# A new hand-written order for a convolution and SwiGLU kernel: transfers among the products, two splits later, another joined list

## The chip, the cores and the metric

The kernel runs on one core of one Trainium2 chip. The metric is the device time of one execution in microseconds (us). Three runs of the kernel before gave 2442.12, 2444.2 and 2449.53 us, median 2444.2. One more execution was profiled; it took 2447.03 us.

## The reference

`x` is (8, 4096, 192) in float32. Part one is a causal convolution over the sequence with 7 taps, one set of softmaxed taps for each of 8 heads (24 channels a head). Part two is a feed-forward block on the 32768 resulting rows of 192, with a hidden size of 1536:

```python
w = softmax(weight, axis=-1)                     # (8 heads, 7 taps)
out[b, s, h, :] = sum_k w[h, k] * x_pad[b, s + k, h, :]
x = out.reshape(32768, 192)
xn = x / sqrt(mean(x * x) + 1e-6) * rms_g
g, val = xn @ w_gate, xn @ w_val                 # 192 x 1536 each
y = (g * sigmoid(g) * val) @ w_out               # 1536 x 192
```

## The kernel before, in words

**Pairs.** The 32768 rows are done in 32 pairs of token blocks, two blocks of 512 rows each. Pair 0 and most of pair 1 have code of their own; pairs 2 to 31 all run the same program, shifted from pair to pair.

**Products.** Both matrix products of a pair are done by a scheme that saves products for sums (7 block products in the place of 8, and a like one for the gate and value product). What a program of a pair issues on TensorE is a list of 110 words, `LINE`. 68 gate words come first (`P1.0`, `Aa.1`, ...): each is six products of 64 x 128 weights with 512 columns (L948), three parts of a weight piece against three parts ("splits") of the tokens. The letters name the product, the digit one of six groups of hidden rows. Then 42 output words (`o1.1`, ...) follow, each twelve products (L976), which sum up in accumulators X, Y and Z.

**Ring.** The gate weights' 48 pieces (192 KB) of a pair are read again from DRAM for every pair, through a ring of 12 slots. When the last word that reads a slot has been issued, `ring_load` (L822) puts the load of the next piece into that slot on SP's queue. So a ring load waits for TensorE, and what is put on SP's queue behind it waits as well.

**Order by hand.** Nothing is planned at run time. `run` walks through `FIRST` (pair 1), `SECOND` (pair 2) and `ORDER` (pairs 3 on, one walk for each) and issues each word as it comes; every engine works its own words in this order, and waits where data or a buffer are missing. `p3` issues three words of `LINE`. Every other word names an engine (A ScalarE, V VectorE, G GpSimd, S the SP queue) and an act; a `+` behind it means one pair ahead, `++` two, `-` one pair behind:

- `f1`, `f3` (ScalarE copies), `f4`, `f5`, `f6` (VectorE sums, L1018 and L1025): from one bank of products to the next; `ga` to `gd`: silu of a bank (L1031), `ma` to `md`: silu times value (L1038), into the tiles `ht`; after both, the bank is free.
- `h1` to `h4` (L1003): the sums of `ht` that the output words read. `o6.j` reads `h2.j`, `o7.j` reads `h3.j`.
- `c1`, `s7`, `c2` (copies), `C22`, `C21` (sums, L1055), `T11` to `T22` (transposes into `o_sb`, L991), `st` (stores, L1087): the output. `C22` and `C21` free or change the accumulators that following words need.
- `cv0` to `cv6` (L470 on ScalarE for tap 0, else L474): the taps of the convolution, over all 128 partitions; `sq`, `red`, `pow`, `bc`, `mul`: the normalisation, of which GpSimd does `pow` and `mul` (L524).
- `pl` (put_away, L1098): eight transfers of the normalised rows to DRAM; `ft` (fetch, L676): four transfers back, turned, into the tokens `xb`; `ld` (load_part, L174): eight loads, one a head, of x for the convolution of the pair after, into the one buffer `xh` that `pl` has just emptied.
- `x1` to `x4` (L868): sums of the tokens; `n`, `l`, `d` (L705 on ScalarE, L854, L856): the three splits of the five token operands 0 to 4.

The walk is short to state:

```python
for word in words:
    p = w + word.count("+") - word.count("-")
    if word[0] == "p":
        for _ in range(int(word[1:].rstrip("+-"))):
            if p in pairs:
                next(pairs[p].line)
    ...
    else:
        eng, name = word[0], word[1:].rstrip("+-")
```

A product bank is one of four pairs of PSUM banks. `open` takes the first free one in the order in which `g`, `m`, `C21`, `T11` and `T12` gave them back, so the order of the words also settles which word waits for whose bank.

In `FIRST`, the token operands of pair 2 still lie where the ring's slots will be (the operand that the trace calls `ring`), so `R`, the start of the ring, waits for the last split that reads them, `Vd.0+`.

Of the kernel before, what the change touches and what calls it, by code (L numbers as in the profile page):

```python
# [20 lines left out]
def kernel(  # L21
# [58 lines left out]
    )  # L80
    ORDER = (
# [15 lines left out]
    )  # L97
    SECOND = (
# [15 lines left out]
    )  # L114
    FIRST = (
# [14 lines left out]
    )  # L130
    LINE = (
# [7 lines left out]
    )  # L139

    cst = ctx.enter_context(tc.tile_pool(name="cst", bufs=1))
# [1213 lines left out]
```

## Time and profile before

| | |
|---|---|
| median of 3 runs | 2444.2 us (2442.12 to 2449.53) |
| profiled execution | 2447.03 us |
| its span, first to last instruction | 2445.2 us |
| TensorE busy | 2427.2 us, 99% |
| VectorE busy | 2089.3 us, 85% |
| ScalarE, GpSimd busy | 1034.0 us, 565.7 us |
| DMA | 430.55 MB, 176 GB/s on average |
| mean granted TensorE clock | 0.999 |

The profile gives, for one execution, each engine's busy time; the chain of work that ended last, followed back from the last instruction; a timeline of every engine; and, for every idle stretch, what ended it. PE is TensorE's products and PEld its weight loads, DVE VectorE, ACT ScalarE, POOL GpSimd, SPq the queue of SP that asks for DMAs. L948 is line 948 of the kernel. "issue" is time in which an engine waited for nothing that the profile shows. The ends of the products are modelled, and some of their records can be missing.

### The profile page before, as it was taken

The page shows a single profiled execution, that of the slowest core. Times are in us where ns is not written, and L with a number is a line of the kernel's source. Part 1 is how long each engine was busy: PE and PEld are TensorE (multiplying, and loading weights), DVE is VectorE, ACT ScalarE, POOL GpSimd, SP SyncE. Part 2 cuts the span into 40 slices and gives each one's busy share as a digit, 9 for nine tenths or more (in the row PEclk, how much of TensorE's full clock was granted, in tenths as well). Part 3 has the DMA queues.
Part 4 walks back from the last instruction along what each step waited for, and adds up shares of the span by engine and source line. Part 5 has one row for each costly group of instructions (what it writes and reads, how often), then busy time and mean ns, then how long its engine had stood idle before and what let it go on. Part 6 is the DMA issues. An engine that isn't in the chain of part 4 may idle for free.

```text
span 2445.2 us, 69382 instructions
## 1 busy us (share of the span) xinstructions
PE 2427.2 (99%) x29136; PEld 1978.5 (81%) x29136; DVE 2089.3 (85%) x2702; ACT 1034.0 (42%) x1431; POOL 565.7 (23%) x482
## 2 busy tenths in 40 slices
PE   8999999999999999999999999999999999999998
PEld 5647888888888888888788898888888788888886
DVE  9678888889888899888898888898888898888974
ACT  6443344444344444344444444443444443444432
POOL 0542122211222211222211222211222112222111
PEclk9999999999999999999999999999999999999999
DMA  7375678777788677778677787777786777876753
GB/s 153 61 212 145 168 177 215 191 170 176 171 186 216 184 170 173 173 196 206 177 173 171 173 210 194 173 175 171 179 215 181 169 173 172 197 204 179 175 155 83
DMA packets 716392, 430.55 MB, mean 176 GB/s; under 512 B 510330, under 2 KB 702386, under 8 KB 716082
## 3 DMA queue, kind: packets, MB, share of 16 engines
q1 hardware_dynamic: 712336, 425.21, 70.7%
q8 instruction: 230, 3.77, 0.7%
q10 hardware_dynamic: 3746, 0.92, 0.2%
q14 instruction: 80, 0.66, 0.1%
HBM read 366.96 MB, written 58.98 MB: 174 GB/s over the span
## 4 chain that ended last, share of the span: by engine, by line
PE 97%; DVE 1%; DMA 1%; SPq 1%; issue 0%; ACT 0%; DVEq 0%; ACTq 0%
PE ps L948 57%; PE ps L976 35%; PE ps L920 2%; PE ps L1135 2%; SPq L174 1%; DMA ht<-in_moe_w_val_dram 0%; DVE part L854 0%; DMA x<-in_x_dram 0%; DVE ht L1003 0%; DMA xh<-in_x_dram 0%; DMA ht<-in_moe_w_gate_dram 0%; SPq L258 0%; DVE part L856 0%; DVE y L474 0%; DVE ht L1038 0%
## 5 line engine op out<-in xcount | busy, mean ns | idle before, releaser
L948 PE MATMUL ps<-part,ring 64*128 64x512 f32 x11160 | 1305.3, 387 | 0.1
L948 PEld LDWEIGHTS ps<-part,ring 64*128 64x128 f32 x11160 | 1108.5, 184 | 161.7 <-issue 5.6
L1031 ACT ACTIVATE tt<-ps 128x512 f32<-128x512 f32 x744 | 441.8, 598 | 683.8 <-PE ps L948 614.8
L1038 DVE TENSOR_TENSOR ht<-ps,tt 128x512 f32<-128x512 f32 x744 | 497.7, 685 | 208.8 <-ACT tt L1031 200.2
L976 PE MATMUL ps<-ht,wo_sb 128*32 128x384 f32 (+2 forms) x7272 | 430.3, 380 | 0.0
L976 PE MATMUL ps<-ht,x 128*32 128x256 f32 (+2 forms) x6696 | 413.1, 379 | 2.8 <-DVE ht L1003 2.6
L976 PEld LDWEIGHTS ps<-ht,wo_sb 128*32 128x32 f32 x7272 | 321.5, 110 | 94.7 <-issue 12.6
L976 PEld LDWEIGHTS ps<-ht,x 128*32 128x32 f32 x6696 | 298.4, 110 | 86.5 <-DVE ht L1003 3.2
L474 DVE SCALAR_TENSOR_TENSOR y<-xh,tp,y 128x1536 f32<-128x1536 f32 x186 | 337.2, 1813 | 3.9 <-ACT y L470 3.5
L503 POOL TENSOR_SCALAR r<-r 128x8 f32<-128x8 f32 x31 | 6.2, 198 | 1431.7 <-DVE r L498 1431.6
L1025 DVE TENSOR_TENSOR ps<-ps,tt 128x1024 f32<-128x1024 f32 x210 | 258.3, 1230 | 36.9 <-ACT tt L705 24.8
L705 ACT COPY ps<-ps 128x1024 f32<-128x1024 f32 (+1 forms) x151 | 134.0, 887 | 274.6 <-PE ps L948 130.1
L1003 POOL TENSOR_TENSOR hs<-ht 128x512 f32<-128x512 f32 x120 | 155.8, 1298 | 169.3 <-DVE ht L1038 127.9
L705 ACT COPY tt<-ps 128x384 f32<-128x384 f32 (+1 forms) x182 | 151.9, 835 | 89.6 <-PE ps L976 79.6
L705 ACT CAST part<-tt 128x1024 fp32r<-128x1024 f32 x60 | 62.8, 1047 | 287.4 <-DVE tt L868 287.4
L1003 DVE TENSOR_TENSOR ht<-ht 128x512 f32<-128x512 f32 x252 | 168.6, 698 | 6.8 <-PE ps L976 6.6
L1003 POOL TENSOR_TENSOR ht<-ht 128x512 f32<-128x512 f32 x120 | 154.4, 1299 | 2.3
L976 PE MATMUL ps<-hs,x 128*32 128x256 f32 (+2 forms) x2232 | 145.2, 379 | 0.0
L948 PE MATMUL ps<-part,part 64*128 64x512 f32 x912 | 128.8, 386 | 0.0
L976 PEld LDWEIGHTS ps<-hs,x 128*32 128x32 f32 x2232 | 106.3, 110 | 24.1
L856 DVE SCALAR_TENSOR_TENSOR part<-part,xb 128x1024 fp32r<-128x1024 f32 x87 | 105.6, 1214 | 0.0
L854 DVE TENSOR_TENSOR part<-xb,part 128x1024 fp32r<-128x1024 f32 x87 | 103.3, 1214 | 0.0
(137 smaller groups left out, 1619.4 us busy)
## 6 DMA issues: line engine op xcount, KB each, us to landing
ring<-wd SPq DMA_DIRECT2D x1326, 192.0 KB
xb<-xd SPq DMA_DIRECT2D x60, 512.0 KB
xd<-xh SPq DMA_DIRECT2D x240, 96.0 KB
part<-wd SPq DMA_DIRECT2D x114, 192.0 KB
xh<-in_x_dram SPq DMA_DIRECT2D x192, 105.0 KB
xb<-xd SPq DMA_DIRECT2D x60, 256.0 KB
out_dram<-o_sb SPq DMA_DIRECT2D x126, 96.0 KB
out_dram<-o_sb SPq DMA_DIRECT2D x62, 128.0 KB
```

Of the source, the lines that this page charges most:

```text
L474: nc.vector.scalar_tensor_tensor(out=y, in0=xk, scalar=w, in1=y, op0=ALU.mult, op1=ALU.add)
L705: nc.scalar.copy(out=dst, in_=src)
L854: e.tensor_tensor(out=split_of(g, 1).bitcast(F32R), in0=src, in1=high, op=ALU.subtract)
L856: nc.vector.scalar_tensor_tensor(out=split_of(g, 2).bitcast(F32R), in0=high, scalar=1.0 + SPLIT, in1=src, op0=ALU.mult, op1=ALU.subtract,)
L920: nc.tensor.matmul(out=self.both(j, c)[:, h, :], lhsT=wf[HALF[h], k, 2 * HOME[j] + f, :], rhs=rb[HALF[h], k, g, :], start=(k == 0), stop=( ...
L948: nc.tensor.matmul(out=self.both(j, c)[:, h, :], lhsT=left[HALF[h]], rhs=right[HALF[h]], start=(first and q == 0), stop=True, skip_group_c ...
L976: nc.tensor.matmul(out=self.acc(b)[i * Q : (i + 1) * Q, at : at + n], lhsT=left, rhs=cols, start=fresh, stop=True, skip_group_check=True, ...
L1003: engine[eng].tensor_tensor(out=dst, in0=a, in1=b, op=op)
L1025: nc.vector.tensor_tensor(out=self.both(j, c), in0=self.both(j, "b"), in1=s5, op=ALU.add)
L1031: nc.scalar.activation(out=tt[:, t, :], in_=self.both(j, c)[:, 0, :], func=AF.Silu)
L1038: nc.vector.tensor_tensor(out=self.hv(j, "abcd".index(c)), in0=self.both(j, c)[:, 1, :], in1=tt[:, t, :], op=ALU.mult,)
L1135: nc.tensor.matmul(out=bank(h, bks[h])[:], lhsT=wf[HALF[h], AT[h][k], u * NF + f, :], rhs=xb[HALF[h], g, k, :], start=(k == 0), stop=(k == ...
```

## The change

Only the lists are new. In `ORDER` and `SECOND`:

- The eight loads of x (`Sld`) stand behind words 54 to 61 of a pair, before behind 60 to 90. The puts (`Spl`) and fetches (`Sft`) stand behind words 45 to 54, before behind 42 to 62, and the four fetches follow the last put almost at once.
- Eight of the ten stores (`Sst`) of a pair stand later, several of them among the output words of the next pair.
- Tap 5 goes from the head of the next walk to the end of this one; `T11` goes from the output words to the head of the next walk; `Vl.4` is done at the end, and `Vd.4` at the head, before the other way round. `C21` stands in front of tap 4, before behind it.
- One word of the last pair's list, not three, is left for the head of the walk. Many acts stand some words sooner or later, and some output sums (`h`) change places.

In `FIRST`, `Vd.1+` and `Vl.2+` go from in front of `Vmd.5` to behind `Vh2.5`. In `LINE`, neighbours among the gate words change places, and the output words come in another order; the words are the same 110.

```diff
@@ -79,38 +79,38 @@
         "o3.3 o3.1 o3.0 o3.5 o3.2 o3.4",
     )
     ORDER = (
-        "p3- p1 Vcv5+ Af1.0 p1 VT12- p1 VT21- p1 Vcv1+ VT22- Aga.1 p1 Vma.1 Vl.4 p1 Aga.0 p1",
-        "Af3.0 Vma.0 p4 Vf4.0 p1 Agb.1 Sst0.1- p3 Vcv2+ Vmb.1 p2 Vf5.0 Sst0.2- Agc.0 p1 Vmc.0",
-        "Agd.1 p2 Vmd.1 Agd.0 p2 Agb.0 p1 Vcv6+ Vmb.0 Sst0.3- Vmd.0 p1 Vcv3+ Af1.2 p1 Sst1.0-",
-        "p1 Agc.1 Vmc.1 p1 Sst0.4- Af3.2 Vf4.2 p3 Sst0.0- p1 Aga.2 Sst1.1- p1 Vma.2 Vf5.2 p1",
-        "Asq+ Agc.2 p1 Vred+ p1 Vmc.2 Agd.2 p2 Agb.2 p1 Vmd.2 Gpow+ Agb.3 p1 Vmb.2 p1 Af1.4",
-        "Vmb.3 Vbc+ p2 Gmul+ Aga.3 p1 Spl.4+ p1 Af3.4 Vma.3 p2 Vf4.4 Spl.2+ p1 Spl.7+ Aga.4",
-        "p1 Vma.4 Vh1.1 Spl.5+ p2 Vf5.4 Spl.1+ p1 Agd.3 Vmd.3 Sst1.3- p2 Gh1.0 Agc.4 Spl.3+",
-        "Vmc.4 p1 Spl.0+ Agd.4 p1 Af1.5 Sst1.4- Gh1.3 Agb.4 Gh3.0 Spl.6+ Vmd.4 p1 Gh3.1 Vmb.4",
-        "p2 Sft.0+ Af3.5 Sft.2+ p1 Sft.4+ Gh1.2 p2 Vf4.5 Sld.4++ p2 Sft.5+ Aga.5 Vma.5",
-        "Sld.3++ p1 Agc.3 p1 Vf5.5 Gh3.3 Gh1.4 Vh3.2 p1 Sld.7++ Vmc.3 p2 Vf6.5 Agc.5 p2 Agb.5",
-        "Agd.5 Sld.6++ p1 Vmb.5 p1 Vmd.5 Vmc.5 p1 Vh1.5 Sld.5++ p1 Gh3.4 Vh2.0 Sst1.2- p3 Ac1",
-        "p1 Vh2.3 An.0+ Vh3.5 p2 Vh2.2 Gh2.1 p1 Vx3+ Sld.0++ Vh2.4 p2 Vd.0+ An.1+ p1 Vl.1+",
-        "Vl.0+ p1 Sld.2++ Vx1+ Vh2.5 Vx2+ p2 An.3+ As7 Vh4.2 Vh4.0 Vh4.3 p2 VT11 p1 An.2+ p1",
-        "Vh4.4 Sld.1++ p1 Vh4.1 Vd.2+ p1 Vh4.5 Vl.2+ Vl.3+ Ac2 p2 Vd.1+ p3 Vx4+ p2 An.4+ p1",
-        "Vd.3+ Acv0++ p1 VC22 Vd.4+ Vcv4++ p5 VC21",
+        "VT11- p1- p2 Af1.0 VT12- Vcv6+ VT21- p2 Aga.1 p1 VT22- p1 Vma.1 p2 Vd.4 p1 Aga.0",
+        "Af3.0 p1 Vma.0 p2 Vf4.0 p2 Agb.1 Vcv1+ p2 Agd.1 Vmb.1 p1 Vf5.0 p1 Vmd.1 Agc.0 p1",
+        "Vmc.0 p2 Agd.0 Agb.0 Vcv2+ Vmd.0 p2 Af1.2 p1 Agc.1 Vmb.0 p2 Sst0.2- p1 Vcv3+ p1",
+        "Vmc.1 Af3.2 p1 Vf4.2 Aga.2 Vma.2 p3 Vf5.2 Asq+ Vred+ p3 Agd.2 Agc.2 Vmd.2 p1 Agb.3",
+        "p1 Agb.2 p1 Vmc.2 Vmb.3 Vmb.2 p4 Af1.4 p1 Sst0.3- Aga.3 Gpow+ Vbc+ p2 Vma.3 Gmul+ p1",
+        "Gh1.0 Spl.2+ p1 Spl.0+ Sst1.3- Af3.4 Vf4.4 p2 Sst1.4- Spl.4+ Aga.4 Agd.3 Vma.4 p1",
+        "Vf5.4 p2 Agc.4 Vmd.3 p1 Spl.3+ Spl.5+ Spl.1+ p1 Spl.6+ Gh1.2 Spl.7+ Vh3.2 Agd.4 p1",
+        "Sft.0+ Vmc.4 Vmd.4 Sft.2+ Sft.4+ Sld.2++ Af1.5 Sld.1++ Sft.5+ p1 Agb.4 Gh3.0 Sld.7++",
+        "Vh1.1 p2 Sld.0++ Vmb.4 Gh1.4 Gh1.3 Sst1.1- Sst0.4- p1 Af3.5 p1 Sld.6++ Aga.5 Vf4.5",
+        "Sld.4++ Gh3.4 Vma.5 Gh3.1 p2 Sld.5++ Sld.3++ p2 Vf5.5 Agc.3 p3 Agc.5 Vmc.5 Vmc.3",
+        "Vf6.5 p2 Gh3.3 Agb.5 p2 Agd.5 p4 An.0+ Sst1.0- Vmb.5 p1 Vmd.5 p1 Sst0.0- Vh1.5 Vh2.4",
+        "p1 Ac1 Vh3.5 Vh2.3 Vx1+ Vh2.5 Sst1.2- p1 Vl.0+ Vh2.0 Vx2+ p1 An.1+ p3 Vx3+ Vh2.2",
+        "Vd.0+ p1 An.3+ As7 Vl.3+ p3 An.2+ p3 Sst0.1- Vh4.5 p1 Gh2.1 Vd.2+ p1 Vh4.3 Vl.1+ p1",
+        "Ac2 Vl.2+ Vh4.2 p1 Vh4.1 Vd.3+ p1 Vx4+ p2 An.4+ Vd.1+ p4 Vh4.0 Vh4.4 VC22 p1 Acv0++",
+        "p1 Vcv5++ p2 VC21 Vcv4++ p4 Vl.4+",
     )
     SECOND = (
...
     )
     FIRST = (
         "p1 Vcv5+ W p2 Vcv6+ p1 Aga.0 Vma.0 p2 Asq+ W W p1 Agb.0 W Vmb.0 W p1 Vred+ p2 Agc.0",
@@ -122,20 +122,20 @@
         "Vmb.3 p1 Sft.2+ p1 W p1 Sft.4+ Agc.3 W W W Sft.5+ Vmc.3 p1 W W p1 Agd.3 p1 Vmd.3",
         "Vh1.3 p1 W p1 W W Vh3.3 W p1 Aga.4 W Vma.4 p3 Agb.4 W Vmb.4 p1 W p2 Agc.4 Vmc.4 p1",
         "Gx3+ p1 Vx1+ Agd.4 An.1+ p1 Vmd.4 Vx2+ Vh1.4 p2 Gx4+ Vh3.4 p1 Aga.5 Vma.5 An.3+ p1",
-        "An.2+ p1 Vd.3+ p1 Agb.5 Vd.2+ Vmb.5 Sld.0++ p1 Vl.3+ p2 Vl.1+ Agc.5 Vmc.5 Vd.1+ p1",
-        "Sld.1++ Vl.2+ p6 Sld.2++ Agd.5 p1 Vmd.5 Gh2.0 Gh2.4 Gh2.2 Gh2.3 Gh2.1 p1 Vh1.5 p2",
-        "Ac1 Sld.3++ Vh3.5 Vh2.5 Sld.4++ Sld.5++ Sld.6++ Sld.7++ Acv0++ An.0+ An.4+ Gl.0+",
+        "An.2+ p1 Vd.3+ p1 Agb.5 Vd.2+ Vmb.5 Sld.0++ p1 Vl.3+ p2 Vl.1+ Agc.5 Vmc.5 p1 Sld.1++",
+        "p6 Sld.2++ Agd.5 p1 Vmd.5 Gh2.0 Gh2.4 Gh2.2 Gh2.3 Gh2.1 p1 Vh1.5 p2 Ac1 Sld.3++",
+        "Vh3.5 Vh2.5 Vd.1+ Vl.2+ Sld.4++ Sld.5++ Sld.6++ Sld.7++ Acv0++ An.0+ An.4+ Gl.0+",
         "Vd.0+ p4 Vh4.5 p1 Vh4.0 R p3 As7 p6 Ac2 Vh4.3 Vcv1++ Vcv2++ p8 Vh4.2 p2 Vh4.1 p2",
         "VC21 p1 Vh4.4",
     )
     LINE = (
-        "P1.0 Aa.1 Ea.1 Ba.1 P2.0 Q1.0 P5.0 P6.0 Ab.1 Eb.1 Bb.1 Ad.1 P3.0 P7.0 Q2.0 Ed.1 Bd.1",
-        "Q3.0 Q4.0 P4.0 P1.2 Ac.1 Bc.1 Ec.1 P5.2 P6.2 Q1.2 P2.2 Ab.3 P7.2 Eb.3 Q2.2 P3.2 Q4.2",
-        "Q3.2 P4.2 Bb.3 P1.4 Aa.3 Ba.3 Ea.3 P5.4 P6.4 Q1.4 P2.4 Ad.3 Bd.3 P7.4 Ed.3 P3.4 Q2.4",
-        "Q4.4 P1.5 P4.4 Q3.4 P5.5 P6.5 Q1.5 P2.5 Ac.3 Bc.3 Ec.3 P7.5 Q4.5 Q2.5 P3.5 P4.5 Q3.5",
-        "o1.1 o1.0 o1.2 o1.4 o1.3 o1.5 o7.2 o7.3 o7.4 o2.1 o7.1 o7.5 o6.3 o2.2 o2.3 o2.0 o2.5",
-        "o2.4 o7.0 o6.2 o6.4 o6.1 o6.5 o4.1 o6.0 o4.0 o4.4 o5.4 o5.5 o5.0 o5.2 o4.5 o5.1 o5.3",
-        "o4.3 o4.2 o3.4 o3.3 o3.1 o3.0 o3.2 o3.5",
+        "P1.0 Aa.1 Ea.1 Ba.1 P2.0 Q1.0 P5.0 P6.0 Ab.1 Eb.1 Bb.1 Ad.1 P7.0 P3.0 Ed.1 Bd.1 Q2.0",
+        "Q4.0 Q3.0 P4.0 P1.2 Ac.1 Bc.1 Ec.1 P5.2 P6.2 Q1.2 P2.2 Ab.3 P7.2 Q2.2 Bb.3 P3.2 Q4.2",
+        "Q3.2 Eb.3 P4.2 Aa.3 P1.4 Ba.3 Ea.3 P5.4 P6.4 P2.4 Q1.4 Ad.3 Bd.3 P7.4 Ed.3 Q2.4 P3.4",
+        "Q4.4 P1.5 Q3.4 P4.4 P5.5 P6.5 P2.5 Q1.5 Ac.3 Bc.3 P7.5 Ec.3 Q2.5 P3.5 Q3.5 Q4.5 P4.5",
+        "o1.1 o1.5 o1.4 o1.2 o7.1 o1.3 o7.0 o1.0 o7.4 o7.2 o2.1 o7.5 o2.3 o7.3 o2.5 o6.4 o6.5",
+        "o6.3 o4.2 o2.2 o6.0 o2.0 o6.2 o6.1 o2.4 o4.1 o4.0 o5.5 o5.4 o5.2 o5.1 o5.0 o5.3 o4.5",
+        "o4.4 o4.3 o3.3 o3.1 o3.0 o3.5 o3.2 o3.4",
     )
 
     cst = ctx.enter_context(tc.tile_pool(name="cst", bufs=1))
```

30 rows, old and new, of the table SECOND are left out of this document.

## The prediction

> **What bounds the kernel now.** I read the page, the chain that ended last in order of time, the waits, and the timeline of single engines, in this order. Line 1 of the page says that TensorE is the bound, with VectorE next:
>
> ```profile
> PE 2427.2 (99%) x29136; PEld 1978.5 (81%) x29136; DVE 2089.3 (85%) x2702; ACT 1034.0 (42%) x1431; POOL 565.7 (23%) x482
> ```
>
> The chain shows how little of the rest there is to win. Its columns are start, length and what; two rows make a pair of token blocks (L948 the products into the gate banks, L976 the output products):
>
> ```profile
> 288.36 46.50 PE ps L948 x408
> 334.86 27.44 PE ps L976 x337
> 362.30 46.51 PE ps L948 x408
> ```
> ```profile
> 1472.71 46.93 PE ps L948 x408
> ...
> 1918.84 47.15 PE ps L948 x408
> ...
> 2363.68 46.53 PE ps L948 x408
> ```
>
> An undisturbed pair takes 362.30 - 288.36 = 73.94 us, TensorE back to back. From 288.36 to 2363.68 are 28 pairs in 2075.32 us, and 28 x 73.94 is 2070.32, so all that 28 pairs lose to waits is 5.0 us. The change keeps the 68 + 42 product words of a pair (one word is one group of products in the list), so 73.94 stays the floor: only these 5.0 us and the start are to be won, and all else can only be lost.
>
> Part of the 5.0 us is of one kind, seen here in the same view:
>
> ```profile
> 1173.68 1.82 DVE y L474
> 1175.50 0.48 DVE tt L1055
> 1175.98 0.04 issue
> 1176.02 47.15 PE ps L948 x408
> ```
> ```profile
> ACT y L470 <- DMA xh<-in_x_dram: 5.0, 5, 2.0
> ```
>
> The second fence is a line of the waits (us in total, times, longest). x for two pairs ahead landed late; tap 0 on ScalarE (L470) and the next tap on VectorE (L474) ran late; C21 (L1055), which stands behind that tap, released its bank late; the next pair's first product waited. The three gate rows of this kind are longer than 46.51 by 0.64, 0.42 and 0.64 us: 1.7 in all. The other 3.3 us lie mostly among the output products, where the weight loader waits for nothing that the profile names:
>
> ```profile
> 1903.69 4.69 PEld L976 LDWEIGHTS ps<-ht,x 128*32 128x32 f32 x87 [0.91 <-issue]
> ```
>
> At the start TensorE waits twice for VectorE. These are the timelines of GpSimd, VectorE and TensorE there (start, length, engine, what; in brackets the wait before):
>
> ```profile
> 184.48 9.71 POOL L1003 TENSOR_TENSOR ht<-hs,ht 128x512 f32<-128x512 f32 x5 [7.53 <-PE ps L976]
> ```
> ```profile
> 186.83 0.68 DVE L1038 TENSOR_TENSOR ht<-ps,tt 128x512 f32<-128x512 f32 x1
> 187.43 1.71 DVE L856 SCALAR_TENSOR_TENSOR part<-part,ring 128x1024 fp32r<-128x1024 f32 x1
> 189.06 2.30 DVE L854 TENSOR_TENSOR part<-ring,part 128x1024 fp32r<-128x1024 f32 x1
> 191.29 0.68 DVE L1038 TENSOR_TENSOR ht<-ps,tt 128x512 f32<-128x512 f32 x1
> 192.00 1.07 DVE L1003 TENSOR_TENSOR hs<-ht 128x512 f32<-128x512 f32 x1
> 193.10 1.64 DVE L1003 TENSOR_TENSOR ht<-ht 128x512 f32<-128x512 f32 x1
> 194.85 2.67 DVE L1003 TENSOR_TENSOR ht<-hs,ht 128x512 f32<-128x512 f32 x1
> 197.44 1.21 DVE L856 SCALAR_TENSOR_TENSOR part<-part,ring 128x1024 fp32r<-128x1024 f32 x1
> ```
> ```profile
> 194.80 1.51 PE L976 MATMUL ps<-ht,x 128*32 128x384 f32 x24 [1.35 <-DVE ht L1003]
> 197.57 4.76 PE L976 MATMUL ps<-ht,x 128*32 128x384 f32 x84 [1.26 <-DVE ht L1003]
> ```
>
> 1.35 + 1.26 = 2.61 us of TensorE time.
>
> **First pair: two splits later.** The rows at 187.43 and 189.06 are Vd.1 and Vl.2, which move behind Vh2.5 (194.85). Then Vmd.5 starts at 187.43, Vh1.5 at 188.03 (0.60 on, as from 186.83 to 187.43), Vh3.5 at 189.13 (1.10 on, as from 192.00 to 193.10), ending at 190.8, and Vh2.5 ends at 190.9 + 2.67 = 193.5. TensorE, not held, wants them at 194.80 - 1.35 = 193.45 and 197.57 - 2.61 = 194.96: both waits go. Late next is GpSimd: the last of its five sums (Gh2.1, end 184.48 + 9.71 = 194.19) feeds the word o6.1 between the two, wanted at 193.45 + 0.65 = 194.10. Some 0.1 to 0.2 us come back, and I take 2.4 us gained; the ends are 2.6, if GpSimd's sums run quicker, and 1.5, if they end a microsecond later. The moved splits, 1.71 + 2.30, end at 197.5, where Vd.0 starts now (197.44), so the first ring loads, which wait for Vd.0, stay where they are. The words that read Vl.2 and Vd.1 are the third and fourth of pair 2, behind six output words more.
>
> The rows show both engines slowed: sums of one form and size last 1.07 to 2.67 on VectorE, and 9.71 / 5 = 1.94 on GpSimd. The Trainium skill (SBUF — State Buffer, "SBUF: two separate sides") says that a VectorE operation with two SBUF inputs and a GpSimd operation that reads SBUF lock each other out for a whole instruction. The rows agree in kind; by that rule GpSimd's sums, meeting two VectorE sums more than before, would end some 0.2 us later, and the gain would be 2.2.
>
> **Steady part, VectorE.** A pair's operations are the same ones; Vd.4 and Vl.4 change places, tap 5 goes to the end of the list, and T11 behind the pair's end. I laid both lists beside the words of the products and went along the tight waits with these rows of VectorE:
>
> ```profile
> 1251.07 0.64 DVE L991 STREAM_TRANSPOSE o_sb<-ps 128x256 f32<-128x256 f32 x2
> ...
> 1254.97 1.20 DVE L854 TENSOR_TENSOR part<-tt,part 128x1024 fp32r<-128x1024 f32 x1
> 1256.10 0.68 DVE L1038 TENSOR_TENSOR ht<-ps,tt 128x512 f32<-128x512 f32 x1
> 1256.70 1.22 DVE L1025 TENSOR_TENSOR ps<-ps,tt 128x1024 f32<-128x1024 f32 x1
> 1257.83 1.81 DVE L474 SCALAR_TENSOR_TENSOR y<-xh,tp,y 128x1536 f32<-128x1536 f32 x1
> ```
> ```profile
> 1319.59 0.56 DVE L1055 TENSOR_TENSOR tt<-ps,tt 128x384 f32<-128x384 f32 x1
> ```
>
> This pair starts at 1176.02 + 47.15 + 27.44 = 1250.61. At the head of the new list, from 0.2 after the last output word, stand T12, tap 6, T21 and T22: 3 x 0.64 + 1.81 = 3.7 us. Then ma.1, split d.4, ma.0 and f4.0: 0.68 + 1.20 + 0.68 + 1.22 = 3.8, so f4.0 ends at 7.7. The word that needs it is the thirteenth, at 12 x 46.51 / 68 = 8.2. (Before, f4.0 ended at 1256.70 + 1.22, 7.3 after the start.) No wait, 0.5 us to spare.
>
> In the output stage VectorE never idles, so its end is a sum of rows. C22 stands at 1319.59 and ends 69.5 us after the pair's start; the word that needs its bank comes at 46.51 + 36 x 27.44 / 42 = 70.0. In the new list one product (mc.5, 0.60) and T11 (0.6) leave the stretch ahead of C22, which starts some 0.5 later, behind f6.5: C22 comes 0.6 us sooner. C21, now ahead of tap 4 (1.81), comes about two sooner. The other tight waits (f4.2, Vmb.0, Vmd.3 and their like) keep the same operations ahead of them. So I add 0 for VectorE, ScalarE and GpSimd, bounded by the margins: nothing gained, and a few tenths a pair if one of them is short.
>
> **Steady part, SP's queue.** Moved are the eight loads of x (words 60 to 90 of 110, now 54 to 61), the eight puts and four fetches of the next tokens (42 to 62, now 45 to 54) and most stores (11 to 54 of the next pair, now some in its output stage). All stand among the ring loads, each of which waits for TensorE to free a slot. First two rows of SP, start and length, then one of the chain:
>
> ```profile
> 1292.97 0.86 SPq L676 DMA_DIRECT2D xb<-xd  x2
> ...
> 1313.98 3.02 SPq L174 DMA_DIRECT2D xh<-in_x_dram  x3
> ```
> ```profile
> 1167.45 4.32 DMA xh<-in_x_dram
> ```
> ```profile
> 1260.00:1270.00 10.00, 10.00 (x92) 8.57 (x90) 9.04 (x10) 5.04 (x8) 0.00 (x0) 1.00 0.85 231
> ...
> 1305.00:1315.00 10.00, 10.00 (x190) 8.47 (x186) 10.00 (x16) 2.85 (x4) 0.00 (x0) 1.00 0.95 152
> ```
>
> (The last two are stretches; they end with the clock, the DMA share and GB/s.) The puts wait for GpSimd's scaling, whose place in its queue I find unchanged, and the fetches for the puts: now asked for 42.4 us after the pair's start (1292.97), then within a microsecond of that. Queued behind them are ring loads from word 54 on, all for the next pair, 20 us and more ahead of use. The last load of x is asked for at up to 1317.0, 66.4 us; with five ring loads (192 KB at 231 GB/s, 0.83 us each) and a store now behind the loads of x, at about 61.5. Tap 0 wants x at some 67. With the longest landing on the chain, 4.32, a lateness of up to 2 us becomes 1 to 4 us to spare: the 1.7 us go. The bytes are the same and the DMA share stays near 1 about as long, so I leave the 3.3 us of nameless waits alone (ends: 0 and -3.3).
>
> The later stretch moves 152 GB/s at a share of 0.95, the earlier one 231 at 0.85. The Trainium skill (DMA: Bandwidth & Descriptors, "Specifications") puts line rate at 512 bytes and up, and the rows of x are 96 bytes: a rule against asking for x near the ring's loads. The two rows agree with it; it stands beside rival 3.
>
> **Sum.** 2.4 + 1.7 = 4.1 us less. Against the profiled execution (2447.03 us: span 2445.2 and 1.8 around it) that is 2442.9. It lies 2.8 above the median of the three runs, 2444.2 (2442.12 to 2449.53), so I forecast 2440.1.
>
> **Rivals.** (1) The change does only part of what it says: the start gains, but x lands as late as before, because the DMA queues set it and not SP: 2444.2 - 2.4 = 2441.8; or Gh2.1 holds the start too, 2444.2. For it: the share is near 1 from 42 us on either way. Chance 0.22. (2) All waits go: 2444.2 - 2.4 - 5.0 = 2436.8. Against it: the nameless waits sit in the stage that keeps its DMA load and gets stores added. Chance 0.05. (3) Slower: the second fetch lands late. The sum x1 needs it and now runs six operations (6 x 0.60) behind f6.5, at about 51.4 us, five sooner than before. VectorE has no idle time behind it, so what it waits beyond the 1 us that C22 then has to spare is paid by every pair. Two fetches of 512 KB at 231 GB/s, asked for at 42, end at 46.5, or at 51 with the landing of 4.32 added. It decides from 52.4 on: each microsecond later costs 29 x 1 = 29 us, 2469; half of one, 2455. For it: small packets now follow at once. Against it: the fetches stand ahead of them in the queue. Chance 0.15.
>
> **Numbers.** My forecast 0.58, with 2437.5 to 2443 as its own range; with (1) and (2) the range is 2436.5 to 2446, and (3) is left out. A measurement of this kernel tells about 0.3% (7.3 us) from no change. Faster by more than that needs (2) and some luck: 0.05. Slower by it is (3): 0.15. Within: 0.80.
>
> **What would show it.** Right: no waits of 1.35 and 1.26 at L976 near 195 us, and pair 2's products 2.4 us sooner; pair rows of 46.5 and 27.4 throughout; no ScalarE wait for xh at L470; the loads of x asked for by 62 us of a pair; C21 ahead of tap 4. Wrong: gate rows over 46.6 in every pair (a margin fell short); VectorE waiting for xb at L868; TensorE waiting for a DMA at L948; a wait for GpSimd of over 0.5 us near 194 us.

## The result and the profile after

The changed kernel took 2439.63 us (median of 16 runs, 2438.85 to 2440.45), the kernel before, run beside it, 2444.95 us (16 runs, 2442.12 to 2449.53). The ratio is 0.9977, 95% interval 0.9969 to 0.9984: 5.3 us less, between 3.9 and 7.6. The runs also lie closer together, within 1.6 us where they spread over 7.4. The profiled execution took 2440.45 us, 2438.6 of it span.

First the page's row of busy times, then rows of the chain of the changed kernel (start, length, what):

```profile
PE 2423.1 (99%) x29136; PEld 1900.2 (78%) x29136; DVE 2096.1 (86%) x2702; ACT 1032.5 (42%) x1431; POOL 563.0 (23%) x482
```
```profile
285.80 46.52 PE ps L948 x408
332.31 27.44 PE ps L976 x337
...
581.58 12.06 PE ps L948 x102
593.65 0.04 issue
593.69 34.99 PE ps L948 x306
...
877.98 11.86 PE ps L948 x102
889.85 0.04 issue
889.89 35.00 PE ps L948 x306
...
2357.18 46.52 PE ps L948 x408
```

From 285.80 to 2357.18 the 28 steady pairs take 2071.38 us, 1.06 over 28 x 73.94; before it was 5.0. What is left is nearly all in the two gate stages shown, which are longer than the others by 0.6 and 0.4 us. Every output row is 27.44: the nameless waits are gone. Around 195 us there is no wait either. GpSimd's five sums, VectorE and TensorE in turn:

```profile
184.99 8.61 POOL L1003 TENSOR_TENSOR ht<-hs,ht 128x512 f32<-128x512 f32 x5 [7.53 <-PE ps L976]
```
```profile
184.90 1.22 DVE L854 TENSOR_TENSOR part<-ring,part 128x1024 fp32r<-128x1024 f32 x1
186.04 1.28 DVE L1038 TENSOR_TENSOR ht<-ps,tt 128x512 f32<-128x512 f32 x2
187.35 1.71 DVE L1003 TENSOR_TENSOR hs<-ht 128x512 f32<-128x512 f32 x1
189.10 1.66 DVE L1003 TENSOR_TENSOR ht<-ht 128x512 f32<-128x512 f32 x1
190.86 1.59 DVE L1003 TENSOR_TENSOR ht<-hs,ht 128x512 f32<-128x512 f32 x1
```
```profile
193.69 6.00 PE L976 MATMUL ps<-ht,x 128*32 128x384 f32 x106
```

Between the two traces the span falls by 6.6 us: 3.2 at the start (first output products to pair 2's first product, 120.19 to 117.00), 3.9 in the steady pairs, 0.1 at the end, less 0.7 that this execution began its first output products later.

### The profile page after: what moved, and what is told of

It reads as the page before. It is cut to its first block, busy times and chain, and to the rows that moved or that the text cites. A ratio compares the mean times of both kernels' runs of the same rounds, so it can differ in the third digit from the quotient of the medians.

```text
span 2438.6 us, 69319 instructions
## 1 busy us (share of the span) xinstructions
PE 2423.1 (99%) x29136; PEld 1900.2 (78%) x29136; DVE 2096.1 (86%) x2702; ACT 1032.5 (42%) x1431; POOL 563.0 (23%) x482
## 3 DMA queue, kind: packets, MB, share of 16 engines
q8 instruction: 230, 3.77, 0.7%
## 4 chain that ended last, share of the span: by engine, by line
PE 98%; SPq 1%; DMA 1%; DVE 0%; issue 0%; DVEq 0%
PE ps L948 57%; PE ps L976 36%; PE ps L920 3%; PE ps L1135 2%; SPq L174 0%; DMA x<-in_x_dram 0%; SPq L258 0%; DMA ht<-in_moe_w_val_dram 0%; DMA ht<-in_moe_w_gate_dram 0%; SPq L288 0%; SPq L207 0%; DVE o_sb L991 0%; DVE part L324 0%; DVE part L329 0%; DVE y L441 0%
## 5 line engine op out<-in xcount | busy, mean ns | idle before, releaser
L948 PEld LDWEIGHTS ps<-part,ring 64*128 64x128 f32 x11220 | 1056.1, 184 | 219.1 <-issue 5.0
L1038 DVE TENSOR_TENSOR ht<-ps,tt 128x512 f32<-128x512 f32 x744 | 500.9, 687 | 204.9 <-ACT tt L1031 192.8
L976 PE MATMUL ps<-ht,wo_sb 128*32 128x384 f32 (+2 forms) x7272 | 473.9, 380 | 0.0
L976 PE MATMUL ps<-ht,x 128*32 128x256 f32 (+2 forms) x6696 | 443.5, 379 | 0.0
L976 PEld LDWEIGHTS ps<-ht,wo_sb 128*32 128x32 f32 x7272 | 334.7, 110 | 94.8 <-DVE ht L1038 11.3
L1025 DVE TENSOR_TENSOR ps<-ps,tt 128x1024 f32<-128x1024 f32 x210 | 258.6, 1231 | 53.4 <-ACT tt L705 25.5
L976 PE MATMUL ps<-hs,x 128*32 128x128 f32 (+2 forms) x2232 | 131.8, 379 | 0.0
L976 PEld LDWEIGHTS ps<-hs,x 128*32 128x32 f32 x2232 | 97.4, 110 | 27.8
L1003 DVE TENSOR_TENSOR ht<-hs,ht 128x512 f32<-128x512 f32 x151 | 104.2, 692 | 0.4
L948 PE MATMUL ps<-part,part 64*128 64x512 f32 x730 | 103.7, 387 | 0.0
```

The lines of the kernel that those rows point to most:

```text
L948: nc.tensor.matmul(out=self.both(j, c)[:, h, :], lhsT=left[HALF[h]], rhs=right[HALF[h]], start=(first and q == 0), stop=True, skip_group_c ...
L976: nc.tensor.matmul(out=self.acc(b)[i * Q : (i + 1) * Q, at : at + n], lhsT=left, rhs=cols, start=fresh, stop=True, skip_group_check=True, ...
L1003: engine[eng].tensor_tensor(out=dst, in0=a, in1=b, op=op)
L1025: nc.vector.tensor_tensor(out=self.both(j, c), in0=self.both(j, "b"), in1=s5, op=ALU.add)
L1038: nc.vector.tensor_tensor(out=self.hv(j, "abcd".index(c)), in0=self.both(j, c)[:, 1, :], in1=tt[:, t, :], op=ALU.mult,)
```

## The experiments

Theory: the start gains what VectorE's waits cost; the steady pairs gain because SP asks for x sooner. Rivals: the rest of the new order or the joined list (LINE) brings the gain; the DMA queues, not SP, set when x lands; and, for the nameless waits, chance, LINE, or the transfers.

The start stretch and the loss of 28 pairs (their time less 28 x 73.94) are worked out from the starts of products in each trace, as above. "Before" is the median of the kernel before on the same chip. "Behind word 55" below means behind 55 of the 110 words of a pair; the section on the change counts them from 0 and calls this place 54.

| kernel | us, median (range) | before | start | loss |
|---|---|---|---|---|
| before, first trace | 2444.95 (2442.12 to 2449.53) | | 120.19 | 5.00 |
| before, second trace (b1) | 2444.69, one run | 2445.99 | 117.84 | 4.09 |
| changed | 2439.63 (2438.85 to 2440.45) | 2444.95 | 117.00 | 1.06 |
| changed again (a1) | 2439.16 (2438.57 to 2439.93) | 2445.99 | 117.32 | 0.54 |
| before + FIRST (e1) | 2445.03 (2442.94 to 2448.98) | 2447.45 | 117.16 | 5.77 |
| before + the rest (e2) | 2439.31 (2439.00 to 2440.54) | 2447.45 | 118.16 | 0.33 |
| before, loads of x sooner (e3) | 2442.92 (2441.27 to 2443.67) | 2447.45 | 118.04 | 2.68 |
| before, SP's transfers as changed (e6) | 2441.29 (2440.57 to 2444.27) | 2446.87 | 118.25 | 0.28 |
| before + FIRST, loads sooner (e8) | 2441.70 (2440.97 to 2444.06) | 2446.87 | 117.15 | 1.26 |
| changed, loads of x late (e4) | 2494.71 (2490.54 to 2501.96) | 2447.45 | 117.51 | 51.66 |
| changed, fetches late (e9) | 2464.90 (2461.57 to 2466.34) | 2445.99 | 117.19 | 22.93 |
| changed, added packets (e5) | 2463.77 (2456.63 to 2465.78) | 2446.87 | 117.19 | 22.06 |
| changed, loads sooner still (e7) | 2438.85 (2438.54 to 2439.66) | 2446.87 | 117.23 | -0.77 |
| the same again (e10) | 2439.06 (2438.06 to 2439.77) | 2445.99 | 117.24 | 0.19 |

Undisturbed pairs take 73.90 us in some traces and 73.98 in others; the reason is open. Over 28 pairs that is up to 1.1 us either way, so a loss can come out below zero, and differences of a microsecond in the last column say little: of e3's 2.68 us, 1.1 are of this kind.

**The two halves.** In the kernel before, FIRST alone, and all but FIRST:

```diff
 # e1: ORDER, SECOND, LINE as before
-  "An.2+ p1 Vd.3+ p1 Agb.5 Vd.2+ Vmb.5 Sld.0++ p1 Vl.3+ p2 Vl.1+ Agc.5 Vmc.5 Vd.1+ p1",
-  "Sld.1++ Vl.2+ p6 Sld.2++ ...
+  "An.2+ p1 Vd.3+ p1 Agb.5 Vd.2+ Vmb.5 Sld.0++ p1 Vl.3+ p2 Vl.1+ Agc.5 Vmc.5 p1 Sld.1++",
+  "p6 Sld.2++ ... Vh3.5 Vh2.5 Vd.1+ Vl.2+ ...
 # e2: the other way round: FIRST as before, ORDER, SECOND, LINE as changed
```

> The kernel before with only FIRST changed. If the gain at the start is the two waits for VectorE near 195 us alone, the stretch from the first output products to pair 2's first gate products is 117.0 us, as in the changed kernel, and not 120.2; the 28 steady pairs still lose about 5 us as before, some in gate rows over 46.6 and some in output rows over 27.5; the time is 3 us under before. Rival: the start gains only together with the new joined list (LINE), whose first words pair 2 uses; then the stretch stays near 120 and the time is that of before.

> The kernel before with ORDER, SECOND and LINE changed and FIRST as it was. If the two parts are independent, the start keeps its waits of 1.35 and 1.26 us and its 120.2 us, the steady pairs lose about 1 us instead of 5, all output rows last 27.44 us, and the time is 3 to 4 us under before. Rival: the short steady part of the changed kernel was one lucky execution; then output rows over 27.5 come back and the time lies within 2 us of before.

FIRST alone gave the 117.2 us of start that were expected and kept the losses of the steady pairs; ratio 0.9991 (0.9982 to 0.9999), 2.4 us less in the median, with 0.2 to 4.4 in the interval. The rest alone gave the short steady part (0.33 us lost; one output row was 0.5 us longer, for C21); ratio 0.9964 (0.9951 to 0.9978), 8 us against the 2447.45 of before on that chip. In the traces each half does its own part without the other. The times don't show as much: 2.4 and 8.1 us do not add up to the 5.3 of both, measured on another chip, and e2 without the new FIRST (2439.31) was no slower than the changed kernel. But e2's start, with the old FIRST, was 118.16 and not 120.2: its gap is 0.28 us for GpSimd, none for VectorE. That led to b1, below.

**SP's transfers alone, in the kernel before.** e3 moves the loads of x only, e6 puts and fetches as well; in both, every other engine has the lists of before. e8 is e3 with the new FIRST.

```diff
 # e3 (and SECOND alike): loads of x behind words 61 to 66
-  ... Sld.4++ p2 Sft.5+ Aga.5 Vma.5 Sld.3++ p1 ... Sld.7++ ... Sld.6++ ... Sld.5++ ...
+  ... Sld.4++ p2 Sft.5+ Aga.5 Vma.5 Sld.3++ Sld.7++ p1 ... Sld.6++ Sld.5++ p1 ... Sld.0++ Sld.2++ p1 ... Sld.1++
 # e6: Spl, Sft and Sld all at the words of the changed kernel
```

> The kernel before with only SP's order changed: the eight loads of x stand behind words 61 to 66 of a pair instead of 61 to 91; TensorE, VectorE, ScalarE and GpSimd have the same lists as before. Theory of the late x: ScalarE's tap 0 never waits for x, VectorE is never late at the next pair's start, and no gate row is over 46.6 (three were: 46.93 to 47.15), 1.7 us less. The nameless waits among the output products: if they come from loads of x that are asked for during the output products, they go too, and the time is 4 to 5 us under before; if they come from another part of the order, they stay and the time is 1.7 us under before. Rival: the DMA queues and not SP set when x lands; then tap 0 waits as before and nothing is gained.

> The kernel before with the puts, fetches and loads of x, all on SP's queue, at the words of the changed kernel; stores and all lists of the other engines as before. Against the run with the loads alone sooner, puts and fetches are asked for some 2 us sooner too. If the nameless waits come from the busy DMA at the start of the output products, this busy stretch ends before 51 us of a pair, output rows over 27.5 get rarer, and the time is 1 us or so under that run (2442.9, before 2447.5 on that chip). Rival: they hang on LINE, and stay as often as in that run.

> The kernel before with two edits alone: FIRST as changed, and the eight loads of x behind words 61 to 66. If the changed kernel's gain is these two, the time is within 1 us of the changed kernel's (some 2440); the stretch from the first output products to pair 2 is 117.0 to 117.5 us. If the rest of the new order carries part of it (C21 and the tap sooner against the next pair), 2 us are left: some 2442.

With the loads alone sooner, the list of waits no longer names ScalarE's tap 0 waiting for x; one gate row is still over 46.6 (46.83, behind the sums f4.0 and f5.0). The ratio is 0.9982 (0.9973 to 0.9991), 4.5 us less in the median, and the spread falls from 9.4 to 2.4 us. One nameless wait was left in that trace; TensorE's weight loader there:

```profile
712.24 0.15 PEld L976 LDWEIGHTS ps<-ht,wo_sb 128*32 128x32 f32 x3
713.63 1.48 PEld L976 LDWEIGHTS ps<-ht,wo_sb 128*32 128x32 f32 x31 [1.25 <-issue]
```

With puts and fetches moved too (e6) the loss is 0.28 us, as small as in any trace of the changed kernel; ratio 0.9977 (0.9968 to 0.9986). So SP's queue alone gives most of the steady gain; LINE and the lists of VectorE, ScalarE and GpSimd bring none that these traces show. The times leave room for some. e6's trace is its second shortest run of eleven (2440.80 for a median of 2441.29). Its median lies 2.4 us over e7's (below) on the same chip, of which the start explains 1.0, and 2.0 over that of e2, which has the same FIRST and all the new lists, on another chip. Whether the other lists bring the 1.4 to 2 us that are left isn't resolved. e8 came to 2441.7, where the second theory put it: FIRST and the loads are not all of it. Its trace has two nameless waits left, which e6's has not, so part of the rest is the puts and fetches; that C21 and the taps, which this theory named, carry any of it is not shown.

**The loads of x late again, in the changed kernel.** The opposite edit of e3, again on SP alone.

```diff
-  Sft.4+ Sld.2++ Af1.5 Sld.1++ Sft.5+ p1 ... Sld.7++ ... Sld.0++ ... Sld.6++ ... Sld.4++ ... Sld.5++ Sld.3++
+  # behind words 61, 63, 66, 70, 73, 81, 85, 91: Sld.4 .3 .7 .6 .5 .0 .2 .1, as before
```

> The changed kernel with only SP's order changed back in one point: the eight loads of x stand behind words 61 to 91 as before. Theory of the late x: tap 0 on ScalarE waits for x again in a few pairs or more, the split and the taps on VectorE run late, and gate rows over 46.6 come back, where the wait is behind the sum f4.0 (L1025); 2 us or more over the changed kernel. If the nameless waits follow the loads of x, output rows over 27.5 come back too. Rival: the margin comes from the puts and fetches, which stand a little sooner; then the loads can stand late at no cost and the time is that of the changed kernel.

The sign was as the theory has it, the size was not: 55 us more than the changed kernel, for "2 us or more"; ratio to before 1.0194 (1.0174 to 1.0214). Output rows stay at 27.44: the nameless waits do not follow the loads of x. Tap 0 waits for x 26 times; the chain of one such pair shows the way (rows of the waits, then of the chain):

```profile
ACT y L470 <- DMA xh<-in_x_dram: 61.7, 26, 4.7
DVE y L474 <- ACT y L470: 58.8, 26, 4.6
```
```profile
883.26 3.14 DMA xh<-in_x_dram
...
886.55 1.58 ACT y L470
...
888.16 1.82 DVE y L474
...
890.36 1.81 DVE y L474
...
893.22 0.65 DVE o_sb L991 x2
...
893.97 1.00 ACT ps L705
...
895.02 9.34 PE ps L948 x78
```

Above these rows the chain runs through SP's own issuing: loads, ring loads and, between them, the stores that the new order puts among the output words (L1087), up to 882.55. And tap 0 is wanted sooner: it starts 67.15 us into an undisturbed pair, 68.88 before, because VectorE's tap 5 now stands ahead of C21. So the loads are late by more and are wanted sooner, in nearly every pair. The early loads are what the rest of the new order needs, not a gain on top of it.

**The nameless waits.** e9 puts the fetches back behind words 58 to 63, with the loads of x behind them, in the changed kernel; LINE stays new. e5 adds packets.

```diff
 # e9
-  Sft.0+ Vmc.4 Vmd.4 Sft.2+ Sft.4+ Sld.2++ Af1.5 Sld.1++ Sft.5+ p1 ...
+  # behind words 58, 58, 59, 63: Sft.0 .2 .4 .5; behind 61 to 66: the loads
 # e5
+  def more(i, w):   # SP, behind words 66, 68, 70, 72: one head's rows of x to a spare place
+      nc.sync.dma_start(out=zz[i], in_=src)
```

> The changed kernel with the fetches at the words of the kernel before (behind 58 to 63 and not 55) and the loads of x behind them at words 61 to 66; LINE, stores and the lists of the other engines stay. The busy DMA then runs to some 57 us of a pair again, as in the kernel before and in the runs with its fetches. If the nameless waits come from that, output rows over 27.5 are back in some pairs (0.2 to 1.5 us each) and the times spread by 3 us and more, at 2441 to 2444. If they hang on LINE, the output rows stay at 27.44. A third outcome: the fetches come too late for the sum x1 at 51.5 us of a pair, VectorE waits for xb at L868, and every pair is longer, by tens of us in all.

> The changed kernel with added traffic that nothing reads: in every pair SP asks, behind words 66, 68, 70 and 72, for one head's 1024 rows of 96 bytes of x each, into a spare place in DRAM. The output stage of the changed kernel has a DMA share of 0.8 to 0.9, that of the kernel before 1.08 to 1.15 from 48 to 57 us of a pair; the added packets bring it over 1 there. If the nameless waits among the output products come from a busy DMA that lets pages of the instruction queue (q8) land late, output rows over 27.5 come back, a few tenths to 1.5 us in some pairs, each 1.3 to 1.7 us behind the end of a q8 page, and those pages last 1.3 us and more on average from 48 to 57 us. Rival: the nameless waits hang on the list of products (LINE); then the output rows stay at 27.44. In both cases x lands later, and gate rows over 46.6 may come as well, told apart by their place (f1.0 or f4.0, fourth and thirteenth word).

In e9 they are back. A row of the weight loader from e6's list of waits, then two rows of e9's list, and one of e9's nameless waits in its timeline:

```profile
PEld ps L976 <- issue: 11.3, 31, 0.8
```
```profile
PEld ps L976 <- issue: 2.8, 5, 1.0
DVE tt L868 <- DMA xb<-xd: 22.2, 25, 1.8
```
```profile
1690.59 0.22 PEld L976 LDWEIGHTS ps<-ht,x 128*32 128x32 f32 x5
1691.84 0.58 PEld L976 LDWEIGHTS ps<-ht,x 128*32 128x32 f32 x16 [1.04 <-issue]
```

With the old LINE, 31 of these are the short step at the start of each output stage (11.3 us); with the new LINE that step goes by another name, except for one of 0.76 us in pair 0, which every trace has. Without these, the traces whose fetches stand behind words 58 to 63 have 4 (before), 4 (b1), 3 (e1), 1 (e3), 2 (e8) and 4 (e9); the eight traces whose fetches stand behind 55 (changed, a1, e2, e4, e5, e6, e7, e10) have none. Old and new LINE are on both sides. Late loads of x alone (e4) don't bring the waits, and with late fetches they come whether the loads are late (before) or sooner (e3, e8, e9): in these traces it is the place of the fetches that decides. (No run moves the fetches and nothing else.) Rows of the stretches show what goes with it, each 51 to 57 us into a pair, DMA share and GB/s at the end; before, e6, e9:

```profile
1301.60:1307.60 6.00, 6.00 (x118) 4.49 (x113) 6.00 (x8) 2.00 (x3) 0.00 (x0) 1.00 1.16 188
```
```profile
1299.20:1305.20 6.00, 6.00 (x120) 4.58 (x114) 6.00 (x8) 2.12 (x3) 0.00 (x0) 1.00 0.66 134
```
```profile
1312.70:1318.70 6.00, 6.00 (x118) 4.56 (x114) 5.79 (x9) 2.85 (x4) 0.00 (x0) 1.00 1.25 194
```

Over all 28 pairs the share there is 1.12 before and 1.14 in e9, 0.86 in the changed kernel and 0.87 in e6. The profile also lists the packets of the instruction queue (q8): 16 of the 18 waits end 1.3 to 1.8 us behind the end of a q8 packet, the other two, both e9's, 2.0 and 2.5 us. Of all moments from 54 to 63 us of a pair about one in ten lies so. From 51 to 57 us such a packet took 1.4 us on average before and 1.1 in the changed kernel. That the waits are for instructions is argued from this, not shown by an edit; that they go with the place of the fetches is shown. The Trainium skill (Runtime: NRT & Kernel Launch, "Instruction fetch mechanics") says that a sequencer fetches its next 16 KiB block by a DMA queue of its own, mostly hidden. The traces agree on the size (230 packets of q8, 3.77 MB); if these waits are for such blocks, they are not hidden when DMA is this busy.

e9's time is another matter: 25.7 us over a1 beside it, for now VectorE's sums wait for xb (22.2 us, 25 times), x is asked for later too (61.5 to 66.1 us of a pair), and C21 and the taps run late: gate stages lose 12 us, output stages 11, most of it by waits that the profile names. The third outcome came together with the first.

e5 does not tell the theories of the nameless waits apart: the added packets were not done in the stretch that matters (share 0.88 from 51 to 57 us, for 0.86 in the changed kernel, and 0.91 from 66 to 72, for 0.56), and no nameless wait came. What the added transfers cost, 22 us, is not x landing late, for which tap 0 waited in two pairs only. It is the stores. They stand behind the added transfers on SP's queue, and the transposes of the next output wait until a store has emptied `o_sb`. A row of e5's waits:

```profile
DVE o_sb L991 <- DMA out_dram<-o_sb: 21.3, 14, 3.2
```

Fourteen gate stages are longer, by 0.2 to 5.3 us, and each has one of these waits; the changed kernel has none. In the longest one SP was busy with the added transfers until 581.1 us, the stores behind them landed at 585.1, and the transposes began then, 4.5 us into the pair.

**Sooner still.** e7 and e10 are one kernel; a1 is the changed kernel beside e10.

```diff
-  p1 Agb.4 Gh3.0 Sld.7++ Vh1.1 p2 Sld.0++ ... Sst1.1- Sst0.4- p1 ... Sld.6++ ... Sld.4++ ... p2 Sld.5++ Sld.3++
+  # Sld.7 behind word 56, .0 .6 behind 57, .4 .5 behind 58, .3 behind 59; the two stores behind 61 and 62
```

> The changed kernel with the loads of x sooner still: the six that stand behind words 56 to 62 stand behind 56 to 59, and two stores of the pair before go from between them to behind words 61 and 62. Theory of the late x: the two gate rows that still waited (0.63 and 0.45 us, each behind a pair whose last load of x was asked for at over 63 us) become 46.5, and the time is 0.5 to 1 us under the changed kernel. Rival: what is left is set by the landing, not by the asking; then the time is that of the changed kernel.

> The changed kernel with the loads of x sooner still, once more, now on the same chip as the changed kernel itself: 2438.9 as before, 0.5 to 1 us under the changed kernel; rival: no difference of more than 0.3 us.

> The changed kernel itself, for the comparison with the runs beside it: 2439.6 us as before; some gate rows over 46.6 in pairs whose last load of x was asked for late, output rows at 27.44, the start stretch at 117.0 to 117.5.

The late gate rows went (the largest left are 0.14 and 0.11 us; a1 has one of 0.35). In time it is nothing that can be told: 2439.06 against 2439.16 side by side, ratios to before 0.9968 (0.9956 to 0.9981) and 0.9970 (0.9958 to 0.9981). The rival holds: as far as these runs can tell, the steady part of the changed kernel is at its floor.

**The start once more.**

> The kernel before itself, for a second trace of it. Three runs with its FIRST showed 118.0 to 118.3 us from the first output products to pair 2's, its own trace 120.2. If 118.2 is the common case, it shows here, with no wait for VectorE of over 1 us, and the change of FIRST is worth some 1 us as a rule; if 120.2 is, it is worth 3. The steady pairs lose about 5 us again, in other pairs than in the first trace.

The second trace of before has 117.84 us and one wait of 0.28, for GpSimd. First VectorE and GpSimd in the trace before of the prediction, then in b1:

```profile
184.60 2.30 DVE L854 TENSOR_TENSOR part<-ring,part 128x1024 fp32r<-128x1024 f32 x1
```
```profile
185.25 1.22 DVE L854 TENSOR_TENSOR part<-ring,part 128x1024 fp32r<-128x1024 f32 x1
```
```profile
185.37 10.09 POOL L1003 TENSOR_TENSOR ht<-hs,ht 128x512 f32<-128x512 f32 x5 [7.53 <-PE ps L976]
```
```profile
195.51 5.41 PE L976 MATMUL ps<-ht,x 128*32 128x384 f32 x96 [0.28 <-POOL ht L1003]
```

The same split takes 1.22 us when it starts ahead of GpSimd's sums (by 0.12 in b1) and 2.30 when it starts behind them (by 0.12 in the first trace, where they began at 184.48). With that 1.08 VectorE was late for the rest of the stage. In e2, e3 and e6 the split was ahead too, and the start took 118.04 to 118.25. The 120.19 of the prediction's trace is one of five with this FIRST, and the only one of its kind.

## Why the prediction was right, point by point

The forecast was 2440.1 in a range of 2436.5 to 2446, and 2439.63 came. The total was right in part by luck: two terms were wrong in opposite directions.

- **Floor.** Held: rows of 46.5 and 27.44 throughout, and no experiment got under 73.9 us a pair.
- **First pair, 2.4 us: mis-sized.** The step itself was right: both waits go, GpSimd's last sum no longer holds anything (it ended at 193.60, its five sums taking 8.61 us and not the 9.71 that I carried over). But the 2.61 us of waits came from one execution. Four traces with the old FIRST average 118.1 without it, nine with the new one 117.2: worth 0.9 us as a rule, 3.2 between the two traces that were compared. The times of e1, 2.4 us less than before with an interval of 0.2 to 4.4, don't tell 0.9 from 2.4. The Trainium skill (SBUF — State Buffer, "SBUF: two separate sides") has a VectorE operation with two SBUF inputs and a GpSimd operation that reads SBUF lock each other out for a whole instruction; the rows agree, 1.22 us or 2.30 by who starts first. I took one draw of this as fixed.
- **Late x, 1.7 us: right in cause, about right in size.** e3, which asks for x sooner and does nothing else, takes tap 0's waits away; e4 brings them back. Gate rows over 46.6 cost 1.7 us in the first trace of before, 0.9 in b1 and 2.4 in e1, and 1.0 and 0.35 were left in the two traces of the changed kernel. The last load was asked for at 58.7 to 63.8 us of a pair, for "about 61.5", and in five pairs later than the 62 that I named as a sign; tap 0 waited in two of these, by 1.02 and 0.83 us. One link was named wrongly: I ended the path at C21's bank and the next pair's first product. In the first trace that product waited 0.16 us more than in other pairs (0.36 for 0.20), and the 0.64 us of the row of 47.15 lie inside it, behind `md` (L1038) and the sums f4.0 and f5.0 (L1025) up to some eighteen words on. TensorE's weight loader:

```profile
1176.02 3.99 PEld L948 LDWEIGHTS ps<-part,ring 64*128 64x128 f32 x36 [0.36 <-DVE tt L1055]
...
1181.65 2.61 PEld L948 LDWEIGHTS ps<-part,ring 64*128 64x128 f32 x24 [0.27 <-DVE ht L1038]
1184.52 3.26 PEld L948 LDWEIGHTS ps<-part,ring 64*128 64x128 f32 x30 [0.26 <-DVE ps L1025]
1188.17 0.99 PEld L948 LDWEIGHTS ps<-part,ring 64*128 64x128 f32 x10 [0.40 <-DVE ps L1025]
```

  That is the margin of 0.5 us that I gave f4.0: in undisturbed pairs it ends 7.38 us into a pair; gate rows grew where it ended at 8.18 or later, and at 7.66 none did. The two rows left in the changed kernel are the same path, from loads asked for at 63.1 and 63.8 us into the pair ahead. ScalarE and the weight loader there:

```profile
575.83 1.58 ACT L470 ACTIVATE y<-xh,tp 128x1536 f32<-128x1536 f32 x1 [1.02 <-DMA xh<-in_x_dram]
```
```profile
589.95 2.60 PEld L948 LDWEIGHTS ps<-part,ring 64*128 64x128 f32 x24 [0.27 <-DVE ps L1025]
...
593.66 0.56 PEld L948 LDWEIGHTS ps<-part,part 64*128 64x128 f32 x6 [0.43 <-ACT tt L1031]
```

- **Nameless waits, 0 of 3.3 us: wrong.** This is the step that failed. I left them alone because the bytes and the DMA share stayed; the bytes did, but the busiest stretch moved out of the output stage with the fetches, and all of them went. What the runs showed in its place is that these waits, 2.2 to 2.5 us in the three traces with SP's old order, go with the place of the fetches. That some 3 us too few here met 1.5 us too many at the start, and that 2444.2, the median I started from, was 0.75 below that of 16 runs, made the total look better than its working.
- **VectorE, ScalarE, GpSimd, 0: right as far as the traces go.** e6 has the old lists of these engines, and its trace loses as little as the changed kernel's; its times leave 1.4 to 2 us open. C21 came 1.65 us sooner (71.17 for 72.82), for "about two"; x1 started at 51.5, for 51.4.
- **Rivals.** (1), x late whatever SP does, falls with e3 and e6. (2), all waits go, is what the steady part did; I gave it 0.05. (3), the second fetch late, did not happen, but e9 shows its place: with the fetches three to eight words later, and the loads behind them, VectorE waits for xb and the kernel loses 25 us. The larger danger was one that I had not priced: late loads of x under the new order, 55 us (e4).

## What to carry to other kernels

When a kernel is within half a per cent of its floor, take several traces before sizing a wait: here one of the two terms read from a single trace was some three times its usual size. A wait that the profile puts down to nothing can still belong to the order of the transfers: compare when the DMA is busiest with the stage in which the wait falls, and try the transfers' queue alone before touching the engines. And an order in which one engine's step comes sooner needs what feeds it sooner too: test each half without the other. And what is added to a queue can cost most through what stands behind it: e5's four small transfers a pair cost 22 us, through the stores.

## What the runs showed of the hardware

The same VectorE split (L854, 128 x 1024) took 1.22 us or 2.30 us, by whether it started 0.12 us ahead of GpSimd's sums or 0.12 us behind them. Six traces with the DMA share at about 1.1 from 51 to 57 us of a pair held 18 waits of TensorE that no semaphore explains, up to 1.4 us each, and 16 of these end 1.3 to 1.8 us behind the end of a packet of the instruction queue; eight traces with a share of 0.83 to 0.97 there held none.
